# Finding the places of a head's two halves with one search, and moving the sparse slots

## The chip, the cores and the metric

The kernel runs on one core of a Trainium2 chip. Its time is the device time of one execution in microseconds (us). Engines are named as in the profile: PE is TensorE, DVE is VectorE, ACT is ScalarE, POOL is GpSimd, SP is SyncE; L716 is line 716 of the kernel before.

## The reference

Two branches read the same 2048 rows of 512 values and are added to the input. Branch A is attention with 32 heads of 16 that share one key and one value head. Branch B is a mixture of 64 x 64 = 4096 experts with product keys: for every row and each of 32 heads, two score vectors of 64 are formed, the best two of each are taken with their places, the four sums give the best two experts, and these are weighed by a softmax of two.

```python
xn = _layernorm(x, axis=-1)
return x + _A_ref(xn, wq, wk, wv, wo) + _B_ref(xn, w_q, k1, k2, u, v)

# _B_ref, E = 64, K = 2
s1 = jnp.einsum("nhd,ed->nhe", q1, k1)
s2 = jnp.einsum("nhd,ed->nhe", q2, k2)
i1 = jnp.argsort(-s1, axis=-1)[..., :K]
i2 = jnp.argsort(-s2, axis=-1)[..., :K]
cand = (t1[..., :, None] + t2[..., None, :]).reshape(BS, H, K * K)
eidx = (i1[..., :, None] * E + i2[..., None, :]).reshape(BS, H, K * K)
ord2 = jnp.argsort(-cand, axis=-1)[..., :K]
g = _softmax(top_s, axis=-1)
act = _gelu(jnp.einsum("nd,nhkd->nhk", xf, ue))
out = jnp.einsum("nhk,nhk,nhkd->nd", g, act, ve)
```

## The kernel before, in words

The order of all instructions is written out by hand. After a preparation (norms, query and key products, up to about 125 us) a loop of 256 steps runs over the attention: a step `d` makes the scores of two blocks of 128 keys for four heads and 512 rows (`scores`, L450, exponential on ACT at L457) and the products with the values of the two blocks before (`pv`, L467). Everything of branch B is fed into these steps.

On PE, a generator (`score_thread`) is asked in each step for about 3.6 us of further work (`fill`). It makes the expert scores item by item: an item (`item`) is 128 rows and one chunk of four heads, 12 matmuls into one PSUM tile of 512 columns (L701). These columns are four heads, each with its two halves of 64 scores. DVE then takes the eight largest values of each of the eight halves (`max`, MAX8, L714) and finds their places (`max_index`, L716). One `max_index` is two records in the profile: MATCH_VALUE_LOAD loads eight values, FIND_INDEX8 looks for them. Four items are a batch (`batch`, L734 on): DVE adds the best values, POOL turns the places into expert numbers (from the cast at L760 on), and one or two steps later ACT takes the exponential and DVE forms the gates (`gates`, L780 or L811).

There are four phases of 512 rows, each of eight chunks. For phases 0 and 1 the experts' rows are fetched one by one. A *slot* is one choice of one expert for 128 rows: POOL issues an indirect gather (L1181) into one of 12 buffers, DVE makes the dot product with the row (L1193, a custom instruction and a read of its accumulator), and later adds the weighted second half to the sum (`xa`, L1228). There are 512 slots. For phases 2 and 3 all experts are computed (`dense`): the gates are spread by one-hot matrices (DVE compares at L975 to L978, PE at L1013; their transposes are L942), then PE forms all activations (L917) and sums (L1059). The scores come in the order phase 0, a quarter of phase 1, phase 2, then the first dense pass, the rest of phase 1, phase 3, and the second dense pass.

How many slots are taken in a step is set by a few rates at the loop's head (`pos`, L1588): 2.5 a step until the first 32 index sets exist, then 2.3 for the first 20 steps after a dense pass, else 1.75; 2.6 in the first dense pass; in the second what is left, spread evenly over the steps that remain. Within a step DVE does its dots and sums between the two halves of the attention work (`mid`). A batch of the last chunk before a dense pass does its conversions on DVE instead of POOL, because the one-hot part waits for them.

Once, at about 120 us, the kernel branches on a value that it computed: `guard` (L383) loads a flag into each engine's register and runs a part only if it is set. At the end (L542 to L554) the last attention block is normalised and stored.

Of the kernel before, what the change touches and what calls it, by code (L numbers as in the profile page):

```python
# [11 lines left out]
F32 = mybir.dt.float32  # L12
# [11 lines left out]
P = 128  # L24
# [4 lines left out]
E = 64  # L29
# [4 lines left out]
NC = 8  # L34
TPH = GT
# [22 lines left out]


@with_exitstack  # L60
def tile_kernel(ctx, tc, x, wq, wkv, wo, wqT, kT, uv, ub, vb, out):
    nc = tc.nc
    pool = lambda name, **kw: ctx.enter_context(tc.tile_pool(name=name, **kw))
    dram = pool("dram", bufs=1, space=DRAM)
    const = pool("const", bufs=1)
# [3 lines left out]
    small = pool("small", bufs=2)  # L69
# [22 lines left out]
    ident = const.tile([P, P], F32, name="ident")  # L92
# [38 lines left out]
    xtile = lambda name: ps.tile([P, 512], F32, name=name, tag="x", bufs=3)  # L131
# [540 lines left out]
    def wp_read(n, ks=range(KC)):  # L672
        for k in ks:
            wk = wk_tile()
            nc.sync.dma_start(raw(wk[:]), d_w[SEQ[n][1]][:, k])
            WC.setdefault(n, []).append(wk)
# [2 lines left out]
           + [(1, c) for c in range(2, NC)] + [(3, c) for c in range(NC)])  # L679
    M8, I8 = {}, {}  # L680
    BT = 4

    def item(n_, ti, make=()):
        ph, c = SEQ[n_]
        nph, nc_ = SEQ[n_ + 1] if n_ + 1 < len(SEQ) else (None, None)
        t = TPH * ph + ti
        g, j = divmod(t, GT)
        b, jb = divmod(ti, BT)
        if jb == 0:
            m8 = small.tile([P, BT, 8, 8], F32, name="m8", bufs=1)  # L690
            i8 = small.tile([P, BT, 8, 8], U32, name="i8", bufs=1)
            M8[ph, c, b], I8[ph, c, b] = m8, i8
        m8, i8 = M8[ph, c, b], I8[ph, c, b]
        p = xtile("psc")

        more = nc_ is not None and not (ph >= NSP and c == NC - 1)
        read = more and n_ + 1 >= NC
        n = 0
        for k in range(KC):
            for kk, a, bb in LOWS_LAST[n:n + 3] if ti == 0 else [(k, *ab) for ab in TERMS]:  # L700
                nc.tensor.matmul(p, XT[kk][:, a, j * P:(j + 1) * P], WC[n_][kk][:, bb, :],  # L701
                                 start=n == 0, stop=n == 11)
                n += 1
            if read and ti == 0 and k < 2:
                wp_read(n_ + 1, range(2 * k, 2 * k + 2))
            if k < KC - 1:
                yield 3 * UNIT
            if k == 1 or k == 0 and n_ == 1:

                yield from islice(make, 1)  # L710
        if more and nph != ph:
            load_xt(nph, j)
        for s in range(8):
            nc.vector.max(m8[:, jb, s, :], p[:, s * E:(s + 1) * E])  # L714
        for s in range(8):
            nc.vector.max_index(i8[:, jb, s, :], m8[:, jb, s, :], p[:, s * E:(s + 1) * E])  # L716
        if jb == BT - 1:
            batch(ph, c, b)
        yield 3 * UNIT

    IDX, G = {}, {}
# [11 lines left out]
    def batch(ph, c, b):  # L733
        m8, i8 = M8.pop((ph, c, b)), I8.pop((ph, c, b))  # L734
        sh = [P, BT, 4]
        T = lambda name, dt=F32, s=sh, bufs=1: small.tile(s, dt, name=name, bufs=bufs)
        mv = m8.rearrange("p t (h s) k -> p t h s k", s=2)
        a1, a2, b1, b2 = mv[:, :, :, 0, 0], mv[:, :, :, 0, 1], mv[:, :, :, 1, 0], mv[:, :, :, 1, 1]
        s1, c1, c2, cond = T("s1"), T("c1"), T("c2"), T("cond")
        V = nc.vector  # L740
        V.tensor_add(s1, a1, b1)
        V.tensor_add(c1, a1, b2)
        V.tensor_add(c2, a2, b1)
        V.tensor_tensor(out=cond, in0=c1, in1=c2, op=OP.is_ge)
        mx = T("mx")
        V.tensor_max(mx, c1, c2)
# [11 lines left out]
        fi = T("fi", F32, [P, BT, 8, 2])  # L758
        G_ = V if ph >= NSP and c == NC - 1 else nc.gpsimd
        G_.tensor_copy(fi, i8[:, :, :, 0:2])  # L760
        fv = fi.rearrange("p t (h s) k -> p t h s k", s=2)
        i1a, i1b, i2a, i2b = fv[:, :, :, 0, 0], fv[:, :, :, 0, 1], fv[:, :, :, 1, 0], fv[:, :, :, 1, 1]
        e1, e2 = T("e1"), T("e2")
        stt = V.scalar_tensor_tensor
        den = T("den")
        if ph < NSP:
            idx = T("idx", I32, [P, BT, 4, 2], NIDX)
            i1 = fv[:, :, :, 0, :]
            G_.tensor_scalar(i1, i1, float(E), None, op0=OP.mult)
            G_.tensor_add(e1, i1a, i2b)  # L770
            G_.tensor_add(e2, i1b, i2a)
            G_.tensor_add(i1a, i1a, i2a)
            G_.tensor_sub(e1, e1, e2)
            G_.tensor_mul(e1, e1, cond)
            G_.tensor_add(i1b, e1, e2)
            G_.tensor_copy(idx, i1)
            gg = T("gg", F32, [P, BT, 4, 2], NIDX)

            def gates():
                V.tensor_scalar(den, ex, 2.0 * XUP, 2.0 * XUP, op0=OP.mult, op1=OP.add)  # L780
                V.reciprocal(gg[:, :, :, 0], den)
                V.tensor_mul(gg[:, :, :, 1], ex, gg[:, :, :, 0])
                G[ph, c] = gg

            exp_later(gates)
            for jb in range(BT):
                IDX[ph, c, b * BT + jb] = idx[:, jb].rearrange("p h k -> p (h k)")
            return
        w = slice(8 * c, 8 * c + 8)
        if c == 0:  # L790
            DT.clear()
            gated_all.clear()
            dense_tiles()
        df1, df2, dgt = DT[:3]
        ii = T("ii", F32, [P, 2, BT, 8])
        for n, (p0, p1, q0) in enumerate(((i1b, i1a, i1a), (i2a, i2b, i2a))):
            o = ii[:, n].rearrange("p t (h k) -> p t h k", k=2)
            G_.tensor_copy(o[:, :, :, 0], q0)
            G_.tensor_sub(e1, p1, p0)
            G_.tensor_mul(e1, e1, cond)  # L800
            G_.tensor_add(o[:, :, :, 1], e1, p0)
        hi = T("hi", F32, [P, BT, 8])
        G_.tensor_scalar(hi, ii[:, 1], 32.0, -32.0, op0=OP.is_ge, op1=OP.mult)
        for r in range(2):
            G_.tensor_add(df2[:, :, r, w], hi, ii[:, 1])
        G_.tensor_scalar(hi, hi, -2.0, None, op0=OP.mult)
        for r in range(2):
            G_.tensor_add(df1[:, :, r, w], hi, ii[:, 0])

        def gates():  # L810
            V.tensor_scalar(den, ex, 2.0, 2.0, op0=OP.mult, op1=OP.add)  # L811
# [7 lines left out]
            stt(dgt[:, :, 1, w], gg, GS, gh, op0=OP.mult, op1=OP.subtract)  # L819
            if c == NC - 1:  # L820
                gated_all.append(True)

        exp_later(gates)
# [536 lines left out]
    dense_on, quiet = [0], [0]  # L1360
# [94 lines left out]
    with tc.manual_schedule(engines=ENGINES):  # L1455
# [28 lines left out]
        for k in range(KC):  # L1484
# [3 lines left out]
                                           op0=OP.mult, op1=OP.subtract)  # L1488
# [87 lines left out]
    with tc.manual_schedule(engines=ENGINES):  # L1576
# [4 lines left out]
        half = STEPS // 2  # L1581
        pos, since = 0.0, half
        for d in range(half + 24):


            if dense_on[0] != 0:
                since = d
            if dense_on[0] == 1:  # L1588
                pos += 2.6 if d < half * 3 // 4 else max(0.0, NSL - pos) / max(half - 3 - d, 1)
            else:  # L1590
                pos += (2.5 if len(IDX) < NC * TPH else 2.3 if 0 <= d - since < 20 else 1.75, 0, 0.25, 1.5, 0.5)[dense_on[0]]

            todo = max(min(int(pos + 0.001), g_next[0]) - d_next[0], 0) if d else 0

# [58 lines left out]

            norm_steps(d)
            att_steps(d, mid, fill)
        flush()
        run(STORES)
        while a_next[0] < NSL:
# [8 lines left out]


def build(nc, tc, args):
    tile_kernel(tc, *args)  # L1670


def lay_out(A_x, A_wq, A_wk, A_wv, A_wo, B_x, B_w_q, B_k1, B_k2, B_u, B_v):
# [30 lines left out]
```

## Time and profile before

| | us |
|---|---|
| median of 3 timed runs | 1787.16 (1787.01 to 1787.59) |
| the profiled execution, device time | 1783.53 |
| its span, first to last instruction | 1781.7 |
| busy in it: PE | 1690.9 (95%) |
| DVE | 1592.7 (89%) |
| ACT | 1329.0 (75%) |
| POOL | 680.8 (38%) |

The granted clock of PE was 0.994 of full speed over the span. Lines in the prediction are copied from views of the profile. A row of windows gives the stretch, its length, and for each engine the busy time and the number of instructions. A row of waits names the engine, the tile and line that waited, who released it, the total, how often, and the longest. A row of the timeline gives start, duration, engine, line, operation, and in brackets how long the engine sat idle before it and for whom. A row of groups gives busy time and the mean in ns.

### The profile page before, as it was taken

The numbers are of one execution on the slowest core, as the hardware profiler recorded it, in microseconds if no ns is written. First come the engines' busy times: TensorE is split into PE (matmuls) and PEld (weight loads), VectorE is DVE, ScalarE is ACT, GpSimd is POOL, SyncE is SP. The second block draws the span as 40 slices with busy tenths as digits, with TensorE's granted clock in tenths as the row PEclk, the third lists the DMA queues.
The fourth block names the chain that finished last, engine by engine and source line by source line (L and its number), as shares of the span: only waits on it lengthen the run. The fifth ranks groups of instructions, "written<-read, shape, count | busy, mean of one in ns | idle before, by whom it ended". The sixth has DMA issues, their size and how long they took to land.

```text
span 1781.7 us, 35035 instructions
## 1 busy us (share of the span) xinstructions
PE 1690.9 (95%) x11070; PEld 598.6 (34%) x11070; DVE 1592.7 (89%) x6367; ACT 1329.0 (75%) x1793; POOL 680.8 (38%) x893
## 2 busy tenths in 40 slices
PE   7989998999998889999999999999988899999998
PEld 3433333333333333333333333333333333333332
DVE  7748889999999977999998999999999779999995
ACT  6468787877776987888887666666669887777774
POOL 1024444445542002344343554545530124555450
PEclk9999999999999999999999999999999999999999
DMA  7378788999773469999999987767544679999993
GB/s 261 126 235 313 267 280 298 298 331 330 258 264 105 155 214 281 318 318 344 331 334 347 344 278 250 238 223 238 162 140 135 228 229 332 329 322 342 321 309 142
DMA packets 257272, 470.97 MB, mean 264 GB/s; under 512 B 107316, under 2 KB 118596, under 8 KB 257084
## 3 DMA queue, kind: packets, MB, share of 16 engines
q0 software_dynamic: 73728, 268.47, 43.7%
q1 hardware_dynamic: 182940, 199.59, 35.0%
q8 instruction: 87, 1.43, 0.3%
q14 instruction: 101, 0.83, 0.1%
q10 hardware_dynamic: 416, 0.66, 0.1%
HBM read 407.36 MB, written 56.39 MB: 260 GB/s over the span
## 4 chain that ended last, share of the span: by engine, by line
PE 47%; DVE 31%; ACT 8%; issue 4%; DMA 3%; SPq 1%; POOL 0%; ACTq 0%; DVEq 0%; POOLq 0%
PE pv L467 14%; PE sc L450 8%; PE pout L1059 8%; DVE i L716 7%; PE pact L917 7%; PE psc L701 5%; ACT pt L457 5%; DVE m L714 5%; DVE xa L1228 5%; DVE g L1193 4%; DVE oh L975 3%; PE pwo L567 2%; PE pw L646 1%; DVE obs L977 1%; DVE obs L978 1%
## 5 line engine op out<-in xcount | busy, mean ns | idle before, releaser
L457 ACT ACTIVATE pt<-sc 128x1024 f32<-128x1024 f32 x1024 | 990.2, 1026 | 327.6 <-PE sc L450 276.8
L1181 POOL DMA_INDIRECT g<-in_uv_dram,idx x512 | 550.3, 1075 | 867.2 <-DVE xa L1228 398.0
L467 PE MATMUL pv<-pt,vaug 128*32 128x512 f32 x4096 | 496.2, 602 | 0.0
L1228 DVE SCALAR_TENSOR_TENSOR xa<-g,w,xa 128x512 f32<-128x512 f32 x512 | 374.2, 747 | 0.1
L701 PE MATMUL psc<-wk,xt 128*128 128x512 f16 x1536 | 358.0, 381 | 7.8 <-DVE wk L662 4.7
L450 PE MATMUL sc<-qa,kaug 64*128 64x512 f16 x2048 | 323.1, 382 | 39.1 <-ACT pt L457 34.4
L1193 DVE CUSTOM_DVE_ANT_0 g<-g,xa 128x512 f32<-128x512 f32 x512 | 335.1, 684 | 12.6 <-DMA g<-in_uv_dram,idx 12.3
L701 PEld LDWEIGHTS <-xt 128*128 128x128 f16 x1536 | 141.2, 98 | 205.5 <-issue 57.2
L450 PEld LDWEIGHTS <-kaug 64*128 64x128 f16 x2048 | 82.9, 94 | 377.5 <-issue 373.5
L716 DVE FIND_INDEX8 i<-m,psc 128x8 uint32<-128x64 f32 x1024 | 206.9, 226 | 0.0
L467 PEld LDWEIGHTS pv<-pt,vaug 128*32 128x32 f32 x4096 | 107.3, 109 | 253.4 <-issue 253.4
L917 PE MATMUL pact<-xt,wk 128*128 128x512 f16 x768 | 181.9, 382 | 0.0
L1059 PE MATMUL pout<-wk,wd 128*128 128x512 f16 x768 | 175.8, 379 | 0.0
L714 DVE MAX8 m<-psc 128x8 f32<-128x64 f32 x1024 | 146.3, 217 | 6.5 <-PE psc L701 6.2
L1059 PEld LDWEIGHTS <-wd 128*128 128x128 f16 x768 | 73.1, 98 | 92.5 <-issue 8.1
L917 PEld LDWEIGHTS <-wk 128*128 128x128 f16 x768 | 69.1, 98 | 99.5 <-issue 27.1
L975 DVE TENSOR_TENSOR oh<-io,tr 128x2048 f16<-128x2048 f16 x64 | 78.0, 1218 | 4.9 <-PE pg L1013 4.8
L716 DVE MATCH_VALUE_LOAD i<-m,psc 128x8 f32 x1024 | 76.7, 75 | 0.0
L760 POOL CAST fi<-i 128x64 f32<-128x64 uint32 x30 | 8.2, 272 | 147.2 <-DVE i L716 143.7
L1062 DVE SCALAR_TENSOR_TENSOR da<-pout,cols,da 128x512 f32<-128x512 f32 x72 | 53.1, 745 | 6.3 <-PE pout L1059 4.9
L1132 DVE SCALAR_TENSOR_TENSOR gy<-gy,pact 128x512 f32<-128x512 f32 x60 | 40.9, 681 | 17.4 <-ACT gy L1131 17.4
L1131 ACT ACTIVATE gy<-pact,cols 128x512 f32<-128x512 f32 x60 | 41.7, 696 | 15.3 <-PE pact L917 14.4
(227 smaller groups left out, 1458.7 us busy)
## 6 DMA issues: line engine op xcount, KB each, us to landing
wk<-dw SPq DMA_DIRECT2D x96, 256.0 KB
wqt<-in_wqT_dram SPq DMA_DIRECT2D x32, 512.0 KB
un<-in_uv_dram SPq DMA_DIRECT2D x16, 1024.0 KB
ds<-wk SPq DMA_DIRECT2D x64, 256.0 KB
gates<-dg SPq DMA_DIRECT2D x64, 256.0 KB
wk<-ds SPq DMA_DIRECT2D x64, 256.0 KB
dg<-gst SPq DMA_DIRECT2D x14, 928.0 KB
dw<-wk SPq DMA_DIRECT2D x32, 256.0 KB
```

What stands on the lines that cost most here:

```text
L450: nc.tensor.matmul(p[:, b, :], kaug[o:o + 64, kc * P:(kc + 1) * P], QA[u][o:o + 64, i, :], start=True, stop=True)
L457: nc.scalar.activation(PT[u, kc, i], p, AF.Exp, scale=SCALE)
L467: nc.tensor.matmul(PV[u][32 * j:32 * j + 32, :], vaug[:, kc, :], pt[:, b, :], start=kc == 0, stop=kc == 15)
L701: nc.tensor.matmul(p, XT[kk][:, a, j * P:(j + 1) * P], WC[n_][kk][:, bb, :], start=n == 0, stop=n == 11)
L714: nc.vector.max(m8[:, jb, s, :], p[:, s * E:(s + 1) * E])
L716: nc.vector.max_index(i8[:, jb, s, :], m8[:, jb, s, :], p[:, s * E:(s + 1) * E])
L917: nc.tensor.matmul(p, us[:, a, k * P:(k + 1) * P], XT[k][:, c, :], start=n == 0, stop=n == 11)
L975: nc.vector.tensor_tensor(out=oa, in0=num(P), in1=bc(0, tb, P), op=OP.is_equal)
L1059: nc.tensor.matmul(p, wd[0][:, a, j * P:(j + 1) * P], vs[:, c, :], start=n == 0, stop=n == last)
L1181: nc.gpsimd.indirect_dma_start(out=gt, out_offset=None, in_=uv, in_offset=bass.IndirectOffsetOnAxis(ap=IDX[ph, c, ti][:, s:s + 1], axis=0))
L1193: nc.vector.tensor_tensor_reduce(u, u, XN[TPH * ph + ti], scale=1.0, scalar=0.0, op0=OP.mult, op1=OP.add, accum_out=a[:, i:i + 1])
L1228: nc.vector.scalar_tensor_tensor(acc, v, w[:, i:i + 1], acc, op0=OP.mult, op1=OP.add)
```

## The change

A head's two halves are searched together. The eight largest values of the first half are written to places 0 to 7, then those of the second half to places 6 to 13 of a row of 16; the first eight places then hold the best six of the first half and the best two of the second. One `max_index` looks for these eight among the head's 128 scores. Places in the second half come out 64 too high, so a compare and an add take 64 off; a place under 64 means that the value of the second half also stands in the first. Each batch folds the result of the compare into a running maximum (`meet`), and eight steps before the loop's end a flag is made of it (`met_flag`: a reduction, a transpose on PE, a reduction, a compare). After the kernel every engine loads this flag, and if it is set the whole program runs once more with a search for each half (`exact`). The program text holds both versions. The rates of the slots are raised.

```diff
+    SECOND = 8 if exact else 6
+    most = const.tile([P, BT, 4, 2], F32, name="most")
+    nc.vector.memset(most, -float(E))
+
+    def met_flag():
+        m = small.tile([P, 1], F32, name="mm", bufs=1)
+        nc.vector.reduce_max(m, most.rearrange("p t h k -> p (t h k)"), axis=AX.X)
+        p = xtile("pm")
+        nc.tensor.transpose(p[:1, :P], m, ident)
+        r = small.tile([1, 1], F32, name="prd", bufs=1)
+        nc.vector.reduce_max(r, p[:1, :P], axis=AX.X)
+        nc.vector.tensor_scalar(flag, r, 0.0, None, op0=OP.is_ge)
...
         for s in range(8):
-            nc.vector.max(m8[:, jb, s, :], p[:, s * E:(s + 1) * E])
-        for s in range(8):
-            nc.vector.max_index(i8[:, jb, s, :], m8[:, jb, s, :], p[:, s * E:(s + 1) * E])
+            nc.vector.max(m8[:, jb, s // 2, SECOND * (s % 2):][:, :8], p[:, s * E:(s + 1) * E])
+        if exact:
...
+        else:
+            for h in range(4):
+                nc.vector.max_index(i8[:, jb, h, :8], m8[:, jb, h, :8], p[:, h * P:(h + 1) * P])
...
-        G_.tensor_copy(fi, i8[:, :, :, 0:2])
+        for s in range(2):
+            G_.tensor_copy(fv[:, :, :, s, :], i8[:, :, :, SECOND * s:SECOND * s + 2])
+        if not exact:
+            over = T("over", F32, [P, BT, 4, 2])
+            G_.tensor_scalar(over, fv[:, :, :, 1, :], float(E), -float(E), op0=OP.is_ge, op1=OP.mult)
+            G_.tensor_add(fv[:, :, :, 1, :], fv[:, :, :, 1, :], over)
+
+        def meet():
+            if not exact:
+                V.tensor_max(most, most, over)
...
             def gates():
+                meet()
...
-                pos += (2.5 if len(IDX) < NC * TPH else 2.3 if 0 <= d - since < 20 else 1.75, 0, 0.25, 1.5, 0.5)[dense_on[0]]
+                pos += (2.7 if len(IDX) < NC * TPH else 2.5 if 0 <= d - since < 20 else 2.1, 0, 0.25, 1.5, 0.5)[dense_on[0]]
...
+            if d == half - 8 and not exact:
+                met_flag()
...
-    tile_kernel(tc, *args)
+    with tc.tile_pool(name="met", bufs=1) as met:
+        flag = met.tile([1, 1], I32, name="met")
+        tile_kernel(tc, False, flag, *args)
+        again = nc.values_load(flag[0:1, 0:1], min_val=0, max_val=1)
+        with tc.If(again != 0):
+            tile_kernel(tc, True, None, *args)
```

Counted in the two programs: PE's instructions stand in the same order but for the one transpose, ACT has as many as before, and of the 512 slot sums 132 were done when the first one-hot part starts and 148 are now; 360 and 392 at the second.

DVE at the entry to the first one-hot part, before: the last item of the last batch (`m` its largest values, `i` the places, `psc` the PSUM tile), then the batch (`s`, `c`, `cond`, `mx`: sums and comparisons of the best values; `fi` the places as floats; `ii` and `e` the chosen ones).

```order
L714 MAX m_7511<-psc 128x8 x8
L716 MAX_INDEX i_7512<-m_7511,psc 128x8 x8
L741 TENSOR_TENSOR s_7723<-m_7511 128x16
L742 TENSOR_TENSOR c_7724<-m_7511 128x16
L743 TENSOR_TENSOR c_7725<-m_7511 128x16
L744 TENSOR_TENSOR cond<-c_7724,c_7725 128x16
L746 TENSOR_TENSOR mx<-c_7724,c_7725 128x16
L747 TENSOR_TENSOR mx<-mx,s_7723 128x16
L760 CAST fi<-i_7512 128x64
L798 COPY ii<-fi 128x16
```

The same place now:

```order
L727 MAX m_7438<-psc 128x8 x8
L734 MAX_INDEX i_7439<-m_7438,psc 128x8 x4
L758 TENSOR_TENSOR s_7634<-m_7438 128x16
L759 TENSOR_TENSOR c_7635<-m_7438 128x16
L760 TENSOR_TENSOR c_7636<-m_7438 128x16
L761 TENSOR_TENSOR cond<-c_7635,c_7636 128x16
L763 TENSOR_TENSOR mx<-c_7635,c_7636 128x16
L764 TENSOR_TENSOR mx<-mx,s_7634 128x16
L778 CAST fi<-i_7439 128x16x2 x2
L781 TENSOR_SCALAR over<-fi 128x32
L782 TENSOR_TENSOR fi<-fi,over 128x16x2
L825 COPY ii<-fi 128x16
```

Eight searches have become four, one cast two, and a compare and an add have come in. In the other 30 batches the rows from the cast on stand on POOL.

SP at the end of the program, before (`ft` the last block's sums, `rsb` its divisors, `out_dram` the output):

```order
L534 DMA wo<-in_wo_dram 128x2x512 x2
L593 DMA ft<-dpart_176 128x512
L593 DMA ft<-dpart_177 128x512
L593 DMA ft<-dpart_178 128x512
L593 DMA ft<-dpart_179 128x512
L583 DMA out_dram<-da 128x512 x4
L583 DMA out_dram<-xa 128x512 x2
L490 DMA rsb<-e 16x512 x4
L554 DMA out_dram<-ft 128x512 x2
L1700 UNCONDITIONAL_BRANCH
```

And now, up to the first row of the second version:

```order
L535 DMA wo<-in_wo_dram 128x2x512 x2
L1703 TENSOR_LOAD met
L1703 ISA x2
L594 DMA ft<-dpart_180 128x512
L594 DMA ft<-dpart_181 128x512
L594 DMA ft<-dpart_182 128x512
L594 DMA ft<-dpart_183 128x512
L584 DMA out_dram<-da 128x512 x4
L584 DMA out_dram<-xa 128x512 x2
L491 DMA rsb<-e 16x512 x4
L555 DMA out_dram<-ft 128x512 x2
L1704 COMPARE_AND_BRANCH
```

SP loads the flag some steps before its last transfers and branches behind them. PE, ACT, DVE and POOL load it as the last thing before their branch.

More of the change, by code (lines that the diff above doesn't have):

```diff
@@ L60, in tile_kernel @@
 @with_exitstack
-def tile_kernel(ctx, tc, x, wq, wkv, wo, wqT, kT, uv, ub, vb, out):
+def tile_kernel(ctx, tc, exact, flag, x, wq, wkv, wo, wqT, kT, uv, ub, vb, out):
     nc = tc.nc
@@ L689, in item @@
         if jb == 0:
-            m8 = small.tile([P, BT, 8, 8], F32, name="m8", bufs=1)
-            i8 = small.tile([P, BT, 8, 8], U32, name="i8", bufs=1)
+            m8 = small.tile([P, BT, 4, 16], F32, name="m8", bufs=1)
+            i8 = small.tile([P, BT, 4, 16], U32, name="i8", bufs=1)
             M8[ph, c, b], I8[ph, c, b] = m8, i8
@@ L713, in item @@
         for s in range(8):
-            nc.vector.max(m8[:, jb, s, :], p[:, s * E:(s + 1) * E])
-        for s in range(8):
-            nc.vector.max_index(i8[:, jb, s, :], m8[:, jb, s, :], p[:, s * E:(s + 1) * E])
+            nc.vector.max(m8[:, jb, s // 2, SECOND * (s % 2):][:, :8], p[:, s * E:(s + 1) * E])
+        if exact:
+            for s in range(8):
+                o = slice(8 * (s % 2), 8 * (s % 2) + 8)
+                nc.vector.max_index(i8[:, jb, s // 2, o], m8[:, jb, s // 2, o], p[:, s * E:(s + 1) * E])
+        else:
+            for h in range(4):
+                nc.vector.max_index(i8[:, jb, h, :8], m8[:, jb, h, :8], p[:, h * P:(h + 1) * P])
         if jb == BT - 1:
@@ L736, in batch @@
         T = lambda name, dt=F32, s=sh, bufs=1: small.tile(s, dt, name=name, bufs=bufs)
-        mv = m8.rearrange("p t (h s) k -> p t h s k", s=2)
-        a1, a2, b1, b2 = mv[:, :, :, 0, 0], mv[:, :, :, 0, 1], mv[:, :, :, 1, 0], mv[:, :, :, 1, 1]
+        a1, a2, b1, b2 = (m8[:, :, :, o] for o in (0, 1, SECOND, SECOND + 1))
         s1, c1, c2, cond = T("s1"), T("c1"), T("c2"), T("cond")
@@ L756, in exp_later @@
             LATER.append(go)
-        fi = T("fi", F32, [P, BT, 8, 2])
+        fv = T("fi", F32, [P, BT, 4, 2, 2])
         G_ = V if ph >= NSP and c == NC - 1 else nc.gpsimd
-        G_.tensor_copy(fi, i8[:, :, :, 0:2])
-        fv = fi.rearrange("p t (h s) k -> p t h s k", s=2)
+        for s in range(2):
[7 more added lines that the diff above has]
+                V.tensor_max(most, most, over)
         i1a, i1b, i2a, i2b = fv[:, :, :, 0, 0], fv[:, :, :, 0, 1], fv[:, :, :, 1, 0], fv[:, :, :, 1, 1]
@@ L810, in gates @@
         def gates():
+            meet()
             V.tensor_scalar(den, ex, 2.0, 2.0, op0=OP.mult, op1=OP.add)
@@ L1700 @@
     with tile.TileContext(nc) as tc:
-        tile_kernel(tc, *args)
+        build(nc, tc, args)
     r = run(nc, [arrays], core_ids=[0])
```

## The prediction

> **What bounds the kernel now.** The profiled execution took 1783.53 us: its span of 1781.7 us and 1.8 us around it. That is 3.6 us under the median of the three timed runs, 1787.16 us; I work out a difference against the profiled execution and put it on the median. The kernel works in stages, so I read first the windows cut at their borders: preparation, search and sparse slots (130 to 550), first dense pass (its one-hot part 550 to 660, the rest to 1010), search and sparse slots again (1010 to 1310), second dense pass (one-hot to 1430), end.
>
> ```profile
> core 0: us, PE busy (x) PEld busy (x) DVE busy (x) ACT busy (x) POOL busy (x), PEclk, DMA share, GB/s
> 130.00:350.00 220.00, 206.64 (x1282) 73.06 (x1274) 195.52 (x1014) 175.47 (x257) 98.84 (x128) 0.98 0.85 291
> 350.00:550.00 200.00, 196.46 (x1217) 66.43 (x1216) 196.99 (x1277) 150.00 (x205) 100.44 (x188) 1.00 0.83 281
> ...
> 660.00:1010.00 350.00, 335.85 (x2015) 112.79 (x2014) 311.62 (x728) 288.10 (x394) 137.68 (x126) 1.00 0.97 320
> 1010.00:1310.00 300.00, 299.45 (x1823) 101.00 (x1820) 292.89 (x1792) 189.61 (x231) 154.67 (x252) 1.00 0.69 234
> ...
> 1430.00:1740.00 310.00, 308.27 (x1875) 103.98 (x1874) 285.74 (x711) 240.91 (x323) 148.48 (x136) 1.00 0.96 314
> ```
>
> The searches stand in 130 to 550 and 1010 to 1310, and there VectorE is 89%, 98% and 98% busy. But TensorE is idle for only 13.4, 3.5 and 0.6 us of them. A busy TensorE need not be at its peak, so the timeline has to show that its matmuls are not stretched where VectorE is full:
>
> ```profile
> 1201.40 0.63 DVE L1193 CUSTOM_DVE_ANT_0 g<-g,xa 128x512 f32<-128x512 f32 x1
> 1201.72 4.06 PE L701 MATMUL psc<-wk,xt 128*128 128x512 f16 x18
> ...
> 1202.05 0.68 DVE L1193 CUSTOM_DVE_ANT_0 g<-g,xa 128x512 f32<-128x512 f32 x1
> 1202.66 2.06 DVE L1228 SCALAR_TENSOR_TENSOR xa<-g,w,xa 128x512 f32<-128x512 f32 x3
> 1204.65 1.14 DVE L714 MAX8 m<-psc 128x8 f32<-128x64 f32 x8
> 1205.71 0.07 DVE L716 MATCH_VALUE_LOAD i<-m,psc 128x8 f32 x1
> ...
> 1207.16 0.22 DVE L716 FIND_INDEX8 i<-m,psc 128x8 uint32<-128x64 f32 x1
> 1207.30 1.13 DVE L714 MAX8 m<-psc 128x8 f32<-128x64 f32 x8
> ```
> ```profile
> 1744.23 4.06 PE L1059 MATMUL pout<-wk,wd 128*128 128x512 f16 x18
> ```
>
> Eighteen matmuls take 4.06 us in the search stage and 4.06 us in the last pass, where nothing is searched. So TensorE runs at full rate beside the full VectorE. VectorE just keeps up. Easing it pays only where TensorE really stood waiting for it. Those are few places (waits of TensorE by stage: name, total us, times, longest us; in order 130:350, 350:550, the entry to the first one-hot part, the entry to the second):
>
> ```profile
> PE psc L701 <- DVE wk L662: 4.7, 4, 2.0
> PE pwt L659 <- DVE i L716: 3.0, 1, 3.0
> ```
> ```profile
> PE psc L701 <- DVE i L716: 2.2, 2, 1.1
> ```
> ```profile
> PE ptd L942 <- DVE da L808: 1.2, 1, 1.2
> PE ptd L942 <- DVE gy L930: 1.2, 1, 1.2
> PE ptd L942 <- DVE da L819: 1.2, 1, 1.2
> ```
> ```profile
> PE ptd L942 <- DVE da L819: 2.1, 1, 2.1
> ```
>
> They sum to 4.7 + 3.0 + 2.2 + 3.6 + 2.1 = 15.6 us. That is the most the change can win here. The other large wait of TensorE, in 660 to 1010, is for ScalarE, and the change takes no instruction from ScalarE:
>
> ```profile
> PE sc L450 <- ACT pt L457: 13.6, 21, 2.0
> ```
>
> **The change part by part.** *The search.* An item (128 tokens, one chunk of heads) has 8 MAX8 and 8 searches. In the timeline above the 8 MAX8 take 1205.71 - 1204.65 = 1.06 us, and 8 value loads with their searches 1207.30 - 1205.71 = 1.59 us, 0.199 each. Four searches over 128 values replace them. No row shows a search of 128. Two reductions that read the same kind of memory give the slope with length:
>
> ```profile
> 118.19 0.69 DVE L307 TENSOR_REDUCE qmax<-pqs 128x1 f32<-128x512 f32 x1 [4.78 <-PE pqs L305]
> ...
> 119.64 0.27 DVE L374 TENSOR_REDUCE prd<-pm 1x1 f32<-1x128 f32 x1
> ```
>
> (0.69 - 0.27) / 384 = 1.09 ns a value, 0.07 us for 64 more. So I take 0.27 us for a search; the bounds are 0.199 (length costs nothing) and 0.398 (it costs in proportion, nothing saved). An item saves 1.59 - 4 x 0.27 = 0.51 us; 128 items save 65 us of VectorE (0 to 102).
>
> *What is added beside it.* Every batch of four items gets one 128x32 maximum on VectorE. The two batches that enter a one-hot part also get, on VectorE, a second cast, a compare and an add. The nearest rows:
>
> ```profile
> L746 DVE TENSOR_TENSOR mx<-c,c 128x16 f32<-128x16 f32 x32 | 6.0, 189 | 0.0
> ...
> L773 POOL TENSOR_TENSOR e<-e,e 128x16 f32<-128x16 f32 x16 | 6.0, 376 | 0.0
> ```
> ```profile
> L760 DVE CAST fi<-i x2: 186/188/189, 560.9 to 1320.5; 128x64 f32<-128x64 uint32 x2
> ```
>
> 32 x 0.19 = 6 us, and 2 x 3 x 0.19 = 1.1 us. The other 30 batches have the three instructions on GpSimd, at 0.38 each: 1.1 us later per batch, 34 us in all. Cover: before batches GpSimd idles, and the maximum on VectorE comes with the gates, after the exponential, some 5 us behind the cast:
>
> ```profile
> 358.15 0.24 POOL L760 CAST fi<-i 128x64 f32<-128x64 uint32 x1 [3.23 <-DVE c L743]
> ```
> ```profile
> 365.82 0.22 DVE L780 TENSOR_SCALAR den<-ex 128x16 f32<-128x16 f32 x1
> ```
>
> So VectorE's new maximum, which waits for GpSimd's compare, finds it done 6 us before. Queued behind the three instructions on GpSimd are the indices and the next gathers, 1.1 us later; 12 buffers at 2.7 slots a step are four steps of lead, so I cost that at nothing; without this cover it is 1.1 us a batch, 34 us.
>
> *Slots moved.* A slot costs VectorE 0.65 us for its dot (1201.40 to 1202.05), 2.0 / 3 = 0.66 for its sum (1202.66 to 1204.65) and about 0.1 for its small steps: 1.4 us. The rates rise by 0.2 a step early, and by 0.35 a step once the first 32 index sets exist. A step (16 matmuls of L467) and its items (16 records of L716 each) are counted in two windows, of the one line and of the other:
>
> ```profile
> 1050.00:1100.00 50.00, 15.39 (x128) 3.34 (x128) 1.00 0.66 219
> ```
> ```profile
> 400.00:450.00 50.00, 16.75 (x160) 1.00 0.93 332
> ```
>
> Eight steps in 50 us, 6.25 us each, and 10 items, 1.25 a step: the search frees 0.64 us of a step. Of that the slots take 0.28 or 0.49 and the maximum 0.06. VectorE is eased by 0.3 us a step in 130 to 350, and by only 0.1 in 350 to 550 and 1010 to 1310: it stays near 98% there. The last pass has 32 slots less (2.3 a step for 3), 45 us of VectorE, but in 1430 to 1740 TensorE idled 1.7 us in all, so nothing comes of it.
>
> *The waits then.* In 130 to 350 each of the five waits follows one or two steps of lag, so each loses 0.3 to 0.6 us and the item's own 0.5 us on the spot where the search is what it stands behind: I take 3 of 7.7 us (0 to 7.7). In 350 to 550, 1 of 2.2 (0 to 2.2). At the entries the last four items run back to back, 2.0 us shorter; against that stand 0.6 us for the conversion, two maxima of 0.2 where one dot goes or comes (0.65). I take 1.3 of 3.6 and 1.2 of 2.1 (together from a loss of 1.5 to a gain of 5.7).
>
> *The flag.* One transpose is put at the end of step 248 in TensorE's queue, behind a reduction that stands behind the last sum of that step on VectorE. Queued behind it are the next step's scores. The sum that it follows is like this one, the reduction like that of the guard:
>
> ```profile
> 1752.66 0.75 DVE L1062 SCALAR_TENSOR_TENSOR da<-pout,cols,da 128x512 f32<-128x512 f32 x1 [0.26 <-PE pout L1059]
> ```
> ```profile
> 118.91 0.16 DVE L369 TENSOR_REDUCE mm<-qmax 128x1 f32<-128x4 f32 x1
> ```
>
> 0.75 + 0.16 and two hand-overs: 1.1 us of TensorE (0.9 to 2).
>
> *The branch at the end.* The kernel has one such place now, at the guard; the flag is written at 120.36 + 0.20 and the engines go on after it:
>
> ```profile
> 120.36 0.20 DVE L378 TENSOR_SCALAR flag<-prd,cols 1x1 int32<-1x1 f32 x1
> ...
> 121.59 1.06 PE L659 MATMUL pwt<-ident,wt 128*128 128x128 f32 x8 [1.42 <-PEq L383]
> 121.91 0.14 DVE L1577 COPY mm<-mm 32x1 f32<-32x1 f32 x1 [1.34 <-DVEq L383]
> ```
>
> 1.4 us for load, compare and two jumps. At the end the load of SyncE, the last to finish, is done earlier; its jumps stand partly beside the landing of the last stores. I take 1.4 us (0.3, one jump hidden, to 2.8, twice the guard). [...]
>
> Sum: -3 - 1 - 1.3 - 1.2 + 1.1 + 1.4 = -4.0 us: 1783.5 - 4 = 1779.5 us for an execution like the profiled one, 1787.16 - 4.0 = 1783.2 us on the median.
>
> **The rivals.** *Nothing comes of it.* VectorE is refilled by the slots and TensorE was full: each wait only shifts, the gains are halved to 3 us and the two costs of 2.5 us stand. Time 1786.7. For it: the 0.1 us a step; against it: shorter items in front of every one of the waits.
>
> *Slower: the wide search is dearer.* Place: 350 to 550 and 1010 to 1310, with VectorE at 98%. A step gives up 5 x (0.398 - x) us and takes 0.55; at x = 0.29 us for a search nothing is left, and above it VectorE becomes the bound. At x = 0.35 a step is 0.31 us over. The 500 us hold 80 steps, which make 25 us, less the 10 us that VectorE idles there (3.0 and 7.1): 15 us, and with the costs of 2.5, 1804.7. Against it: the slope of the reductions, and 0.27 lies under the point, if by little.
>
> *The program runs twice.* If a value of the second half's two best also stands among the first half's, the flag is set and everything runs again: about 1787 + 1783 = 3570 us. [...] Chance 0.02.
>
> **How the numbers follow.** Forecast (a few us faster) 0.50, nothing 0.33, wide search or a dearer end 0.15, twice 0.02. A measurement of this kernel can tell 0.2%, 3.6 us, from no change. The forecast is only just beyond it, so of its 0.50 some 0.41 lie beyond and 0.09 within; of the 0.33 of nothing, 0.05 come out faster, 0.25 within and 0.03 slower; of the 0.15, 0.02 within and 0.13 slower. Faster 0.46, same 0.36, slower 0.18. The gains' upper ends (15.6 less 1.2) would give 1773, all costs and no gain 1792; 8 in 10 leaves out the tips, the overloaded VectorE and the second run: 1775 to 1791.
>
> **What would show it.** Right: searches 0.27 us apart; TensorE idle in 130 to 350 down from 13.4 to about 10; matmuls still 18 in 4.06 us; VectorE near 98% in 1010 to 1310 and near 80% in the last pass; a TensorE wait of about 1.1 us at the flag. Wrong: TensorE waits for GpSimd's indices or for gathers; searches above 0.29 us; the end more than 3 us longer; or a gain above 15.6 us, which would mean that a full TensorE was in truth held by VectorE.

## The result and the profile after

The changed kernel takes 1838.24 us (median of four runs, 1830.62 to 1839.37); the kernel before takes 1787.38 us beside it (1787.01 to 1788.65). The ratio is 1.0286, 95% interval 1.0264 to 1.0308: 51 us slower, where 4 us faster was forecast. The profiled execution took 1838.65 us, with a span of 1836.9 us, 55.2 us more than that of before.

First, in which stage is it lost? The entry to each one-hot part is a border that both kernels have. The row of the one-hot compare gives both entries (the first and last start of its two semaphore events), of the kernel before and of the changed one:

```profile
L975 DVEq EVENT_SEMAPHORE  x2: 21/21/21, 567.0 to 1327.2; - x2
```
```profile
L1003 DVEq EVENT_SEMAPHORE  x2: 21/21/21, 590.0 to 1379.4; - x2
```

23.0 us are lost before the first entry, 29.2 more before the second, 3.0 behind it. With windows cut at each kernel's own borders (first item to first one-hot part; end of that part to the second; end of the second to the end), before and after:

```profile
core 0: us, PE busy (x) PEld busy (x) DVE busy (x) ACT busy (x) POOL busy (x), PEclk, DMA share, GB/s
67.00:567.00 500.00, 472.92 (x2852) 167.40 (x2852) 443.98 (x2524) 375.07 (x538) 213.86 (x338) 0.99 0.79 269
651.00:1327.00 676.00, 658.92 (x4006) 221.93 (x3998) 626.68 (x2642) 495.97 (x647) 296.23 (x382) 1.00 0.83 277
1411.00:1782.00 371.00, 361.60 (x2178) 121.77 (x2176) 316.38 (x779) 272.62 (x361) 148.48 (x136) 1.00 0.88 288
```
```profile
66.00:590.00 524.00, 481.46 (x2853) 168.04 (x2852) 460.23 (x2050) 375.36 (x542) 248.19 (x405) 0.98 0.80 273
675.00:1379.00 704.00, 665.76 (x4006) 222.75 (x3998) 641.06 (x2264) 496.10 (x650) 321.32 (x436) 0.99 0.83 277
1463.00:1837.00 374.00, 362.70 (x2185) 122.06 (x2181) 280.41 (x665) 272.30 (x354) 114.81 (x108) 1.00 0.77 243
```

TensorE has the same matmuls in each stage (2852, 4006, about 2180), so the stages hold the same work of TensorE. The two stages with searches grew by 24 and 28 us, and VectorE is busier in both (by 16 and 14 us). In the last stage VectorE lost 36 us of work and the stage is no shorter. VectorE's busy time over the whole span says nothing of this; it even fell:

```profile
PE 1690.9 (95%) x11070; PEld 598.6 (34%) x11070; DVE 1592.7 (89%) x6367; ACT 1329.0 (75%) x1793; POOL 680.8 (38%) x893
```
```profile
PE 1710.2 (93%) x11071; PEld 601.3 (33%) x11071; DVE 1585.6 (86%) x5385; ACT 1328.4 (72%) x1793; POOL 701.1 (38%) x983
```

Then, what of VectorE's work became longer? The timeline of VectorE at one item of the changed kernel (start, us, engine, line; eight MAX8 in one row):

```profile
402.15 1.69 DVE L727 MAX8 m<-psc 128x8 f32<-128x64 f32 x8
403.76 0.07 DVE L734 MATCH_VALUE_LOAD i<-m,psc 128x8 f32 x1
403.82 0.29 DVE L734 FIND_INDEX8 i<-m,psc 128x8 uint32<-128x128 f32 x1
...
404.56 0.07 DVE L734 MATCH_VALUE_LOAD i<-m,psc 128x8 f32 x1
404.62 0.29 DVE L734 FIND_INDEX8 i<-m,psc 128x8 uint32<-128x128 f32 x1
404.82 0.67 DVE L1221 CUSTOM_DVE_ANT_0 g<-g,xa 128x512 f32<-128x512 f32 x1
```

Four searches take 404.82 - 403.76 = 1.06 us, 0.265 each: as forecast (0.27). But the eight MAX8, which the change seems to leave alone, take 403.76 - 402.15 = 1.61 us and not 1.06. The item takes 2.67 us for 2.65 before: the MAX8 have eaten the search's gain. The groups of MAX8 over the whole run, before and after (busy us, mean ns of one, idle us ahead and what ended it):

```profile
L714 DVE MAX8 m<-psc 128x8 f32<-128x64 f32 x1024 | 146.3, 217 | 6.5 <-PE psc L701 6.2 <-issue 0.2
```
```profile
L727 DVE MAX8 m<-psc 128x8 f32<-128x64 f32 x1024 | 197.7, 224 | 22.8 <-PE psc L714 4.4 <-issue 0.8
L734 DVE FIND_INDEX8 i<-m,psc 128x8 uint32<-128x128 f32 x512 | 139.1, 290 | 0.0
...
L786 DVE TENSOR_TENSOR most<-most,over 128x32 f32<-128x32 f32 x32 | 5.9, 184 | 0.0
```

One MAX8 is no longer (224 ns for 217); they overlap less (197.7 us for 146.3), and 17.6 us of the idle time ahead of them (22.8 - 4.4 - 0.8) lies in gaps too short for the profile to name what ended them. What they wait for stands in the instructions of the changed kernel, in the order of VectorE's queue, with their semaphore waits:

```
L727 MAX m_1736<-psc 128x8 [waits PE_49]
L727 MAX m_1736<-psc 128x8 [waits DVE_49]
L727 MAX m_1736<-psc 128x8
L727 MAX m_1736<-psc 128x8 [waits DVE_49]
L727 MAX m_1736<-psc 128x8
L727 MAX m_1736<-psc 128x8 [waits DVE_49]
```

Every second half's MAX8 waits for VectorE itself. It writes places 6 to 13, and the first half's MAX8 just ahead of it writes 0 to 7; places 6 and 7 have to be written last by the second, so it waits until the first has finished. In the trace it starts 0.25 us behind its neighbour, once that has ended (a MAX8 of this item lasts 0.21 to 0.23 us), and the next one 0.15 us behind it; before, every MAX8 behind the first of an item started 0.13 to 0.15 us behind its neighbour. (30 of the 1024 waited for VectorE there too, and none was late by it.) The two groups give the price: (197.7 - 146.3) + 17.6 - 0.1 = 69 us over 512 such waits, 0.135 us each.

TensorE's longest groups of waits after (name, total, times, longest) show who pays:

```profile
PE sc L451 <- ACT pt L458: 55.4, 86, 6.5
...
PE psc L714 <- DVE i L734: 9.2, 6, 3.3
PE psc L714 <- DVE wk L663: 8.4, 5, 3.2
```

Before, the same three were 34.4, 2.8 and 4.7 us. The scores now wait longer for ScalarE's exponentials too, though ScalarE's work did not change (1329.0 us busy before, 1328.4 after).

### The profile page after: what moved, and what is told of

It reads as the page before. It is cut to its first block, busy times and chain, and to the rows that moved or that the text cites. A ratio compares the mean times of both kernels' runs of the same rounds, so it can differ in the third digit from the quotient of the medians.

```text
span 1836.9 us, 34136 instructions
## 1 busy us (share of the span) xinstructions
PE 1710.2 (93%) x11071; PEld 601.3 (33%) x11071; DVE 1585.6 (86%) x5385; ACT 1328.4 (72%) x1793; POOL 701.1 (38%) x983
## 3 DMA queue, kind: packets, MB, share of 16 engines
q0 software_dynamic: 73728, 268.47, 42.5%
## 4 chain that ended last, share of the span: by engine, by line
PE 44%; DVE 33%; ACT 7%; issue 4%; DMA 3%; SPq 0%; POOL 0%; DVEq 0%; ACTq 0%; another core or an unknown queue 0%; POOLq 0%
PE pv L468 14%; PE sc L451 8%; DVE m L727 7%; PE pout L1087 7%; PE pact L945 7%; DVE xa L1256 6%; DVE g L1221 5%; DVE i L734 5%; ACT pt L458 5%; PE psc L714 4%; PE pwo L568 2%; DVE oh L1003 2%; PE pw L647 1%; DMA rw<-in_ub_dram 1%; ACT wk L904 1%
## 5 line engine op out<-in xcount | busy, mean ns | idle before, releaser
L1209 POOL DMA_INDIRECT g<-in_uv_dram,idx x512 | 538.7, 1052 | 915.7 <-DVE xa L1256 453.5
L468 PE MATMUL pv<-pt,vaug 128*32 128x512 f32 x4096 | 503.1, 610 | 0.0
L451 PE MATMUL sc<-qa,kaug 64*128 64x512 f16 x2048 | 329.4, 385 | 62.9 <-ACT pt L458 55.4
L1256 DVE SCALAR_TENSOR_TENSOR xa<-g,w,xa 128x512 f32<-128x512 f32 x512 | 372.6, 745 | 0.3 <-DVE w L1244 0.3
L727 DVE MAX8 m<-psc 128x8 f32<-128x64 f32 x1024 | 197.7, 224 | 22.8 <-PE psc L714 4.4
L734 DVE FIND_INDEX8 i<-m,psc 128x8 uint32<-128x128 f32 x512 | 139.1, 290 | 0.0
L1244 DVE SCALAR_TENSOR_TENSOR w<-gth,ga 128x4 f32<-128x4 f32 x128 | 20.6, 161 | 52.5 <-ACT gth L1237 49.5
L1090 DVE SCALAR_TENSOR_TENSOR da<-pout,cols,da 128x512 f32<-128x512 f32 x72 | 53.4, 745 | 13.6 <-PE pout L1087 10.7
L778 POOL CAST fi<-i 128x32 f32<-128x32 uint32 x60 | 12.2, 229 | 122.5 <-DVE i L734 121.7
L1139 DVE SCALAR_TENSOR_TENSOR gy<-gy,gates 128x512 f32<-128x512 f32 x60 | 41.2, 687 | 19.0 <-ACT gy L1161 16.6
```

The source lines that it names most:

```text
L451: nc.tensor.matmul(p[:, b, :], kaug[o:o + 64, kc * P:(kc + 1) * P], QA[u][o:o + 64, i, :], start=True, stop=True)
L468: nc.tensor.matmul(PV[u][32 * j:32 * j + 32, :], vaug[:, kc, :], pt[:, b, :], start=kc == 0, stop=kc == 15)
L727: nc.vector.max(m8[:, jb, s // 2, SECOND * (s % 2):][:, :8], p[:, s * E:(s + 1) * E])
L734: nc.vector.max_index(i8[:, jb, h, :8], m8[:, jb, h, :8], p[:, h * P:(h + 1) * P])
L1209: nc.gpsimd.indirect_dma_start(out=gt, out_offset=None, in_=uv, in_offset=bass.IndirectOffsetOnAxis(ap=IDX[ph, c, ti][:, s:s + 1], axis=0))
L1256: nc.vector.scalar_tensor_tensor(acc, v, w[:, i:i + 1], acc, op0=OP.mult, op1=OP.add)
```

## Experiments

Theory A: the wait of each second half's MAX8 for its neighbour's write takes back what the wide search gives; an item costs VectorE what it did, and the loss is then the 32 slots moved into full stages plus the maxima. Theory B: the loss lies in the additions (maxima, conversions, branch, doubled program) or in the wide search. Eleven kernels were run, in three groups, each beside the kernel before on the same chip (medians of before 1784.2, 1784.4, 1784.8 us).

**The MAX8 in another order.**

```
-        for s in range(8):
+        for s in (0, 2, 4, 6, 1, 3, 5, 7):
             nc.vector.max(m8[:, jb, s // 2, SECOND * (s % 2):][:, :8], p[:, s * E:(s + 1) * E])
```

> The changed kernel with one edit: of an item's eight MAX8 the four of the first halves stand first and the four of the second halves behind them, so that no MAX8 writes places 6 and 7 of a row that the MAX8 just ahead of it has written. Theory A (each second half's MAX8 waits until its partner's write is done, about 0.12 us, 512 times): the eight MAX8 of an item go from 1.60 us to 1.06-1.15 us, and the time from 1838 to 1778-1790 us. Theory B (the loss is in what else was added: the maximum, the conversions, the second program and its branch, the wide search): the eight may shrink, but the time stays at 1825-1838 us.

1784.2 us, ratio 0.9998 (0.9987 to 1.0008): as A expects. The waits are still there, but each is for a write four instructions back, which is done:

```profile
L727 DVE MAX8 m<-psc 128x8 f32<-128x64 f32 x1024 | 146.2, 215 | 7.1 <-PE psc L714 7.0
```

All 51 us go with this one line: without neighbours that overlap there is no loss.

**The overlap put into the kernel before.**

```
-            nc.vector.max(m8[:, jb, s, :], p[:, s * E:(s + 1) * E])
+            nc.vector.max(m8[:, jb, s // 2, 6 * (s % 2):][:, :8], p[:, s * E:(s + 1) * E])
```

(with m8 as rows of 16 and its readers moved to match.)

> The kernel before with the written places alone changed: a head's two rows of m8 share 16 places, and the second half's MAX8 writes places 6 to 13, over the last two that the first half's MAX8 has just written, in the order of before. Searches of 64, rates and the rest are those of before. Theory A (the overlap makes each second half's MAX8 wait for the write of the one ahead): the eight MAX8 go from 1.06 us to about 1.60 us without any wide search, VectorE has 512 x 0.12 = 60 us more to carry in stages where it is nearly full, and the time is 1815-1840 us. Rival (the slower MAX8 came with the wide search or with other code around it): 1.06 us as before and 1782-1788 us.

1843.7 us, ratio 1.0327 (1.0309 to 1.0345), 3.7 us above the expected range: 59 us for 512 waits. The searches are as they were (206.9 us before), the MAX8 are those of the changed kernel, and the two search stages (here 532 and 705 us, for 500 and 676) carry the loss:

```profile
L716 DVE FIND_INDEX8 i<-m,psc 128x8 uint32<-128x64 f32 x1024 | 206.6, 223 | 0.0
L714 DVE MAX8 m<-psc 128x8 f32<-128x64 f32 x1024 | 197.9, 224 | 24.3 <-PE psc L701 6.6
```
```profile
65.00:597.00 532.00, 479.96 (x2853) 168.85 (x2852) 473.09 (x2528) 376.53 (x539) 211.25 (x338) 0.98 0.75 253
681.00:1386.00 705.00, 667.31 (x4002) 222.24 (x3994) 649.73 (x2645) 496.34 (x647) 294.99 (x382) 0.98 0.80 266
```

The wait is made by the places written, not by the wide search.

**The slots alone, and the rest alone.** The new rates in the kernel before; and the changed kernel, MAX8 as it has them, with the old rates:

```
-  2.5 if len(IDX) < NC * TPH else 2.3 if 0 <= d - since < 20 else 1.75
+  2.7 if len(IDX) < NC * TPH else 2.5 if 0 <= d - since < 20 else 2.1
```

> The kernel before with the new rates of slots (2.7, 2.5, 2.1) alone: 32 slots move ahead of the second one-hot parts, 16 of them ahead of the first, and no search is made cheaper. Theory A (VectorE is full in both search stages, so every slot put there lengthens them by its 1.4 us, and the last pass, which TensorE sets, gives nothing back): 1822-1833 us. Rival (VectorE takes the slots in its idle time, and the loss of 51 us has other causes): 1783-1792 us.

> The changed kernel with the rates of slots of the kernel before (2.5, 2.3, 1.75) and nothing else altered: the waits between the MAX8 stay. Theory A (the waits take back what the wide search gives, so an item costs VectorE what it did, and the loss of 51 us is then the 32 moved slots at 1.4 us plus 32 maxima of 0.19 us): 1790-1797 us, no more than 10 us above the kernel before. Theory B (the additions cost the time, not the slots): 1825-1838 us.

1829.4 us, ratio 1.0256 (1.0239 to 1.0272), and 1794.9 us, ratio 1.0061 (1.0047 to 1.0074): both as A expects. The moved slots cost 45.1 us. The trace counts 388 sums in place of 358 ahead of the first compare of the second one-hot part, so 30 slots are moved and not 32 (the counts 360 and 392 are reached only inside that part, and at its end the difference is 28). That is 1.5 us a slot, close to VectorE's time for one (dot, read and sum of before, L1193 and L1228: (335.1 + 42.5 + 374.2) / 512 = 1.47 us); VectorE's busy time in the two search stages grew by 22 and 21 us. Everything else in the change costs 10.7 us (5.9 us of maxima, the flag and the branch, below). Together 55.8, for 51 measured with both. The windows of before with the new rates show the pattern of the changed kernel without any of its searches:

```profile
65.00:582.00 517.00, 476.69 (x2855) 167.54 (x2853) 466.08 (x2592) 376.33 (x543) 231.76 (x354) 0.98 0.82 277
666.00:1369.00 703.00, 667.18 (x4007) 222.65 (x4006) 647.60 (x2699) 497.31 (x651) 311.37 (x397) 0.98 0.84 278
1452.00:1823.00 371.00, 363.35 (x2192) 121.91 (x2184) 281.16 (x663) 272.65 (x355) 114.30 (x108) 1.00 0.77 245
```

17 and 27 us more in the search stages, and nothing back in the last, where VectorE has 35 us less to do.

**The reordered MAX8 with the old rates.** Both edits above, the first forward, the second back.

> The same reordered MAX8, with the rates of slots of the kernel before (2.5, 2.3, 1.75), so that no slot is moved. Theory A: VectorE has about 0.53 us per item to spare in the search stages, which no other engine can use while TensorE sets their length: 1783-1791 us. Theory B: still 25-50 us over the kernel before, 1810-1838 us. If moving slots is what pays once the search is cheap, this run is slower than the reordered kernel with the new rates by 3 us or more.

1776.6 us, ratio 0.9960 (0.9944 to 0.9975): faster than both kernels, and 6.4 us under the range that A expected. That range was wrong: it took TensorE to set the length of the search stages in full. Without the slots the cheaper item does pay, 7.6 us, and the new rates give all of that away. In this run the flag showed a dearer wait than in the changed kernel: TensorE's wait for it, and the timeline of TensorE and two windows behind it:

```profile
PE pm L691 <- DVE mm L689: 4.6, 1, 4.6
```
```profile
1716.90 3.64 PE L468 MATMUL pv<-pt,vaug 128*32 128x512 f32 x16
1720.47 0.94 PE L451 MATMUL sc<-qa,kaug 64*128 64x512 f16 x4
...
1724.04 0.61 PE L451 MATMUL sc<-qa,kaug 64*128 64x512 f16 x4
1724.58 1.92 PE L468 MATMUL pv<-pt,vaug 128*32 128x512 f32 x16
```
```profile
1714.00:1721.00 7.00, 5.37 (x25) 0.94 (x25) 5.65 (x16) 3.16 (x5) 2.25 (x3) 0.53 0.78 258
1721.00:1735.00 14.00, 14.00 (x88) 4.71 (x84) 12.24 (x31) 10.24 (x12) 5.34 (x5) 0.99 0.91 310
```

From 1714 to 1721 us, around and behind the end of the wait at 1715.6, the granted clock is 0.53: sixteen matmuls of `pv` take 3.64 us where soon after sixteen take 1.92. The wait costs 4.6 us and, as an estimate from this clock, up to 0.47 x 7 = 3.3 us more. The length of the wait may be that of this one execution: the same flag cost 1.3 us in the kernel without a second program (below), which has the same work up to there.

**The flag in two parts.** VectorE's maximum over `most` one step earlier than TensorE's transposition:

```
+            if d == half - 9 and not exact:
+                met_most()
             if d == half - 8 and not exact:
                 met_flag()
```

> The kernel with reordered MAX8 and old rates, with the flag in two parts: VectorE's maximum of `most` one step ahead of TensorE's transposition of it. In the run with both in one place TensorE waited 4.6 us there for VectorE. If that wait lies on the path of the last pass, 3-4.6 us go: 1772-1774 us against 1776.6. If the last pass makes it up behind it, 1775-1778 us.

1773.9 us, ratio 0.9939 (0.9925 to 0.9952): the fastest of all, and in the range expected if the wait lies on the path of the last pass. TensorE no longer waits at the flag, and the last stage takes 373 us, for 382 with the flag in one place:

```profile
66.00:561.00 495.00, 471.92 (x2852) 166.92 (x2852) 411.17 (x1986) 373.07 (x536) 230.31 (x389) 0.99 0.79 271
645.00:1319.00 674.00, 658.20 (x3998) 221.53 (x3990) 601.42 (x2210) 494.52 (x645) 304.24 (x421) 0.99 0.83 278
1404.00:1777.00 373.00, 361.23 (x2163) 121.25 (x2161) 315.70 (x781) 272.07 (x360) 148.88 (x136) 1.00 0.86 285
```
```profile
1397.00:1779.00 382.00, 365.77 (x2185) 122.04 (x2181) 316.49 (x781) 273.48 (x361) 149.21 (x136) 0.99 0.85 279
```

The stages of one execution are a weak measure, though: the first search stage of the same two took 495 and 487 us, and the edit changes nothing there. The intervals of this run and of the one before it overlap, so the 2.7 us between them are likely, not shown. Against the kernel before, 10.5 us are.

**No second program.** The read of the flag, the branch and the second program are left out (equal values would not be searched again):

```
-        again = nc.values_load(flag[0:1, 0:1], min_val=0, max_val=1)
-        with tc.If(again != 0):
-            tile_kernel(tc, True, None, *args)
```

> The kernel with reordered MAX8 and old rates, with the read of the flag, the branch and the second program taken off its end (the flag is still worked out, but nothing acts on it, so an input with equal values would not be run again). Theory A (the branch costs its wait at the end and nothing else): 1-2 us less than with them, 1774-1776 us against 1776.6. Rival (a program of twice the length costs all along, through the loading of its code): 5 us or more below, under 1772 us.

1777.1 us (1767.9 to 1784.6), ratio 0.9956 (0.9931 to 0.9980). It lies above both expected ranges, and no difference can be told from 1776.6. The median speaks against a cost of 5 us for the doubled program; the two intervals together are too wide to exclude it. The profile resolves the end better. VectorE's last sums, without the branch and with it (reordered MAX8, old rates), and TensorE's branch over the second program in the latter:

```profile
1768.71 2.47 DVE L554 TENSOR_TENSOR ft<-ft,pwl 128x512 f32<-128x512 f32 x4
```
```profile
1769.70 2.47 DVE L554 TENSOR_TENSOR ft<-ft,pwl 128x512 f32<-128x512 f32 x4
```
```profile
L1704 PEldq COMPARE_BRANCH  x1: 4024/4024/4024, 1770.2 to 1770.2; - x1
```

From the end of these sums to the end of the span are 1774.8 - 1771.18 = 3.6 us without and 1778.7 - 1772.17 = 6.5 us with the branch: 2.9 us, less than the medians of these two runs can tell.

**Other rates.** With the reordered MAX8: half way (2.6, 2.4, 1.9), the first new one alone (2.7, 2.3, 1.75), the later new ones alone (2.5, 2.5, 2.1); and half way with the flag in two parts.

> The reordered MAX8 with rates of slots half way between the old and the new (2.6, 2.4, 1.9). If moved slots cost time by VectorE's work in the search stages, half of the 7.6 us that the new rates cost over the old ones: 1779-1782 us. If that cost is the one wait of 6.3 us of TensorE behind the weights' load in the first dense part, which the new rates bring about, it is there or it isn't: 1775-1778 or 1783-1785 us. If moved slots pay as the change meant them to, below 1775 us.

> The reordered MAX8 with the new rate of slots in the first search stage alone (2.7; then 2.3 and 1.75 as before). With all three new rates the kernel took 1784.2 us, with the old ones 1776.6 us, and TensorE stood once for 6.3 us in the first dense part behind a late load of weights. If that wait comes from the 16 slots that the first rate moves ahead of the dense part, it is here too: 1781-1785 us. If it comes from the later rates, 1774-1778 us.

> The reordered MAX8 with the old rate in the first search stage (2.5) and the new ones after it (2.5, 2.1). If the 7.6 us between old and new rates come from the first stage and the wait in the dense part behind it, 1774-1778 us; if from VectorE's work in the second search stage, where the later rates put their slots, 1780-1785 us.

> The reordered MAX8, the flag in two parts one step apart, and the rates half way (2.6, 2.4, 1.9). The two edits gave 1773.9 us and 1776.4 us by themselves. If both gains hold side by side, 1771-1774 us; if TensorE's work sets the time of both, 1773-1777 us.

| rates, MAX8 reordered | us | ratio to before (95%) |
|---|---|---|
| old | 1776.6 | 0.9960 (0.9944 to 0.9975) |
| half way | 1776.4 | 0.9962 (0.9949 to 0.9976) |
| first new | 1780.4 | 0.9977 (0.9968 to 0.9986) |
| later new | 1786.8 | 1.0015 (1.0003 to 1.0026) |
| all new | 1784.2 | 0.9998 (0.9987 to 1.0008) |
| half way, flag in two parts | 1775.6 | 0.9950 (0.9936 to 0.9965) |

No rate above the old ones pays. Half way and half way with the split flag lie in ranges that were expected (no wait of 6.3 us; gains that do not add); the first new rate alone lies between its two ranges, the later new ones alone above both of theirs. Counted in the profiles (sums at L1256), the first new rate alone has 4 slots more before the first one-hot part than the old rates and 6 more before the second, the half-way rates 8 and 14, the later two alone 10 and 24, all three 16 and 30; so the later two do most of the moving, in both search stages (the first new rate was expected to move 16 ahead of the first part), and the time does not follow the count. With all three TensorE stood once for 6.3 us in the first dense part:

```profile
PE sc L451 <- ACT pt L458: 8.1, 5, 6.3
```

With the first or the later new rates alone no such wait is in the profile, and they still cost 3.8 and 10.2 us. So that one wait is not the whole reason. What is stays open: VectorE is not full on the average (620.3 of 683 us from the first one-hot part to the second with all new rates, 601.7 of 674 with the old). The half-way rates gave nothing clear with the flag in one place (1776.4 us for 1776.6), and nothing with it in two (1775.6 for 1773.9).

## Why the prediction was wrong, point by point

- **The search: right.** 0.265 us measured for 0.27; 0.53 us an item for 0.51.
- **The step that failed** is "An item saves 1.59 - 4 x 0.27 = 0.51 us; 128 items save 65 us of VectorE". It took over the MAX8 at 1.06 us an item because their shapes and number stay. Their places change: the second half's row was moved onto two places that the first half's writes. The waits cost 0.55 us an item, 70 us in all, and the item saves nothing. The diff shows the overlap (`SECOND` is 6 and a MAX8 writes 8), and the wait stands in the order of the changed kernel's instructions; the prediction rests on neither.
- **With that one step put right, VectorE's terms come near the loss.** The moved slots at 45 us (as measured in the kernel before), the maxima 5.9, the item 0.02 x 128 = 3: 54 us more of VectorE, for 52 us that the two search stages grew. That work of VectorE there is paid for nearly in full is what the new rates in the kernel before showed. The prediction's slot of 1.4 us was near (45.1 us for 30, 1.5 each).
- **A second, smaller step failed: the slots at no price.** "VectorE is eased by 0.3 us a step in 130 to 350, and by only 0.1 in 350 to 550 and 1010 to 1310" let the freed time pay for them. With the MAX8 reordered the item does save its 0.53 us, and still the new rates cost 7.6 us, which is all of the gain. Why they do stays open.
- **"Nothing comes of" the slots that leave the last pass: right.** 36 us less of VectorE there (45 were expected), and a stage of 374 us for 371.
- **TensorE's idle time in 130 to 350** was to fall from 13.4 to 10 us. It rose to 16.6 (220 - 203.43):

```profile
130.00:350.00 220.00, 203.43 (x1251) 71.02 (x1247) 193.99 (x808) 170.76 (x253) 110.08 (x149) 0.98 0.86 291
```

- **The slower rival** had the right mechanism (an item that gives less than the slots take, VectorE as the bound in the search stages), with a point of decision at 0.29 us a search. Its cause was another, and its price, 1804.7 us, too low: an item that saves nothing corresponds to a search of 0.398, its upper bound, where its own sum gives 80 x 0.55 - 10 + 2.5 = 36.5 us, 1824. It also counted 350 to 550 and 1010 to 1310 only, while TensorE was behind before 350 already (1251 matmuls in 130 to 350, for 1282).
- **The flag** was to cost 1.1 us (0.9 to 2). It was 0.9 in the changed kernel, but 1.3, 3.0 and 4.6 us in the three runs with the old rates and the flag in one place. VectorE has more to do in the last pass there (316 us busy with the old rates, 280 in the changed kernel), which is the likely reason. The clock of 0.53 around the end of the wait of 4.6 us was not in the sum.
- **The branch at the end** was put at 1.4 us (0.3 to 2.8). It is 2.9 us by the two tails above, and 2.3 in the changed kernel (its sums end at 1831.03 of 1836.9, 5.9 us before the end; before 1778.13 of 1781.7, 3.6): about the upper end of that range, and why was not tested. TensorE's own branch over the second program took 4.0 us (reordered MAX8, old rates), where its branch at the guard of before took 0.23; it lies beside the last stores, which are issued from 1770.4 to 1773.2.
- **"Nothing comes of it"**, the second rival, has the time of the change once the overlap is out of the way: the reordered MAX8 with the new rates took what the kernel before took (ratio 0.9998), where the forecast's sum was 4.0 us less and the rival's 0.5. Its account, gains halved to 3 us against costs of 2.5, is not shown: without the moved slots 7.6 us are gained, and the slots take 7.6 away. A gain of the forecast's size or more is there with the old rates, the half-way ones and the first new one (ratio 0.9977). The rival of a second run did not come about (1838.24 us, one pass); its 0.02 was the author's estimate.

## What to carry to other kernels

When a change packs results closer, look at every writer of the packed tile: where two neighbours on one engine now write a common place, the second may wait for the first to finish, as these MAX8 on VectorE did (0.135 us each time, 69 us in all), although neither's work has changed. Write the rows that overlap some instructions apart; four were enough here (1784.2 us for 1838.2). And do not refill an engine from a forecast saving; measure the saving first, and read the engine's busy time by stage, since a total over the span hides work that moved into a full stage.

## What the runs showed of the hardware

- A MAX8 of 64 values started 0.13 us behind the one ahead (1.06 us for eight), though one lasts 217 ns: neighbours overlap. A MAX8's semaphore wait for the MAX8 just ahead ended the overlap (it started 0.25 us behind) and cost 0.135 us each time; a wait for one four instructions back cost nothing that the group shows (146.2 us for 146.3).
- Around the end of some of TensorE's waits its granted clock was about half for some us: 0.53 from 1714 to 1721 us above, with the wait of 4.6 us, and 0.57 from 380 to 384 us of the changed kernel, behind a wait of only 2.5 us (sixteen `pv` take 3.11 us there). Mean granted clock before and after, over the span:

```profile
core 0: 1781.7 us, clock 0.994
```
```profile
core 0: 1836.9 us, clock 0.984
```

  That is 0.006 x 1781.7 = 11 us of missing clock before and 0.016 x 1836.9 = 29 us after, so a part of the 55 us can lie in matmuls that ran slowly behind waits. How much of it counted is not settled, since VectorE's work set the length of those stages.
